# Another order of the steps, with forty-four on another engine, in a fused linear-attention and two-layer MLP kernel

## The chip, the cores and the metric

The kernel runs on one core of one Trainium2 chip. The metric is device time in microseconds (us), from the start to the end of one execution; lower is better. The core has five engines, each of which runs its own instructions in program order: TensorE (PE in the profile), VectorE (DVE), ScalarE (ACT), GpSimd (POOL) and SyncE (SP), which here only issues DMA transfers. An instruction waits on semaphores until its inputs are there and its output buffer is free, and what stands behind it on the same engine waits too.

## What is computed

Two stages, the second on the output of the first. The first is a recurrent attention with a decaying state of 48 x 48 for each of 4 batches and 8 heads over 768 positions; the second a two-layer MLP on the 3072 tokens, 384 to 2048 to 384, with a smooth ReLU between.

```python
def _attn_ref(r, k, v, w, u):
    for t in range(S):
        cur = np.einsum('bhd,bhe->bhde', u[None] * kt, vt)
        y[:, :, t] = np.einsum('bhd,bhde->bhe', rt, state + cur)
        state = w[None, :, :, None] * state + np.einsum('bhd,bhe->bhde', kt, vt)

def _moe_ref(x, w_in, w_out):
    h = x @ w_in
    g = np.where(h >= 1, h, np.where(h <= -1, 0.0, (h + 1) ** 2 / 4))
    return g @ w_out
```

## The kernel before

**Tiling.** Time is cut into 6 chunks of 128 positions (`C`). A *unit* is one batch in one chunk, so there are 24 units, and a *group* is two units, so there are 12 groups `g`; unit `n` belongs to group `n // 2`. Inside a chunk the recurrence is written as matrix products, and a state per batch is carried from chunk to chunk; groups `g` and `g + 2` share their batches.

**The steps.** Every piece of work is a *step*, a small function registered under a name in the dictionary `do`. For a group or unit, in the order of data:

- `load.K`, `load.R` and `loadV` bring K, R and V in by DMA, issued on SP (384 KB a group; the first two groups in halves of 192 KB). `V` casts V to bf16. `w_in` and `w_out` bring the weights of the MLP in, issued on GpSimd.
- `Ks` and `Rs` scale K and R by tables of powers of the decay (line L327). `KU`, `RKU`, `usum` and `V2` make the diagonal term: K times u, that times R, the sum over each head, and the sum times V (L337, L344, L355 or L357, L369).
- For the first three groups `T` transposes Ks and Rs on TensorE (L388) and `TT` copies the result out of PSUM. Later `KRT` does it with a DMA transpose on SP (L398).
- `A` multiplies R by K on TensorE (L406) and `AT` masks it into SBUF (VectorE L421; for units 0 and 1 ScalarE L412 and GpSimd L416). `Y` multiplies by V and adds the part from the state (L441, L446), and `y` adds the diagonal term on VectorE (L468).
- `Sp`, `Tm` and `decay` update the state (TensorE L432, VectorE L476, GpSimd L489), and `sbf` casts it to bf16.
- `xT` brings `y` into the layout of the MLP: for the first three groups through `X` on TensorE (L501) and a copy, later with a DMA transpose on SP (L511), one for both units.
- `mm1` is the first layer (L526), a quarter `q` of the 2048 columns at a time, 12 matmuls. `relu` and `square` on ScalarE (L534, L539) and `gate` on VectorE (L544) make the smooth ReLU. `mm2` is the second layer (L554), by unit and quarter. `o` copies the result out of PSUM, and `out` stores it from SP (L587). For the last unit the second layer is cut in two column blocks (`mm2` and `rest`), and `ends` copies and stores both.

**The order.** The text `ORDER` lists all 714 steps. A loop at the end of the kernel reads it from left to right and calls each step, and an engine's program order is the order in which its steps are called. A token reads `name.arguments@engine:buffers`: `@A`, `@D` and `@P` put the step on ScalarE, VectorE or GpSimd where it can run on several; the digits behind the colon choose the buffer among those of its kind, and a step that writes to a buffer waits until the last step that used it is done. PSUM has three double banks `h0` to `h2` (for `T`, `A`, `mm1`) and two single banks (for `Sp`, `Y`, `X`, `mm2`). `~n` puts n idle matmuls ahead of a step, and `warm.n` is a step of n idle matmuls. The names of steps and units as used in the text are those of the tokens: `mm1.4.0` is quarter 0 of the first layer for group 4, and `xT.8` the transpose that group 4 needs (units 8 and 9).

The loop:

```python
    for token in ORDER.split():
        token, _, idles = token.partition("~")
        idle[0] = int(idles or 0)
        name, _, bufs = token.partition(":")
        name, _, e = name.partition("@")
        kind, *args = name.split(".")
...
        elif kind in do:
            do[kind](e, [int(x, 36) for x in bufs], *[int(x) if x.lstrip("-").isdigit() else x for x in args])
```

Of the kernel before, what the change touches and what calls it, by code (L numbers as in the profile page):

```python
# [40 lines left out]
usum.1.0@A:1 A.1:0~8 V2.0.0@P:0 Ks.2.0@P:2 AT.2.0:1 loadV.2.0:0 V2.1.0@A:1 Y.0:1 T.3:2 sbf.0@A Tm.2@D usum.0.1@D Y.2:0
TT.3@D:3 y.2:0 AT.1.1:2 Rs.2.0@P:2 A.3:1~14 X.2:0 V2.0.1@A y.0:1 AT.3.0:3 warm.2.h.2 X.0:1 T.5:2~8 AT.1.0 xT.2@A:0
T.4:0 TT.5@D:0 Y.1:0 w_in.1 load.K.3.0:0 xT.0@A:1 sbf.1@A usum.1.1@D A.5:1 mm1.0.0.0:2 KU.2.0@P:0 y.1:2 TT.4@D:1
load.R.3.0:0 V.1.1@A X.1:1 Y.3:0 AT.5.0:0 A.4:0 V2.1.1@P xT.1@A mm1.0.0.1 V.2.0@A:2 Sp.5:1 y.3:0 RKU.2.0@P:0
relu.0.0:0 X.3:0 Tm.5@D:0 mm1.0.1.0:1 AT.4.0:1 xT.3@A decay.5 square.0.0:0 usum.2.0@D:0 Sp.4:1 mm1.0.1.1 w_out.0 Y.4:0
relu.0.1:1 mm1.1.1.-1:0 gate.0.0:0 square.0.1:1 Tm.4@D:1 mm1.0.2.-1:2 relu.1.1:0 Y.5:1 square.1.1:0 V2.2.0@P:0 w_out.1
y.4:1 gate.0.1:1 w_out.2 X.4:0 w_out.3 mm1.0.3.-1:1 xT.4@A:2 gate.1.1:2 relu.0.2:1 Sp.3:0 y.5:2 mm1.1.0.-1:0
square.0.2:1 Tm.3@D KU.3.0@P:1 decay.4 gate.0.2:3 relu.0.3:0 relu.1.0:1 mm2.0.0.0:1 mm2.0.1.0:0 Ks.3.0@P:0
square.1.0:0 KRT.K.3:0 mm1.1.3.-1:2 mm2.0.1.1 Rs.3.0@P:0 RKU.3.0@P:1 mm2.0.0.1 square.0.3:1 gate.1.0:4 mm2.0.1.2 gate.0.3:5
relu.1.3:1 loadV.3.0:1 mm2.0.0.2 mm1.1.2.-1:0 square.1.3:0 usum.3.0@D:1 mm2.0.0.3 relu.1.2:0 KRT.R.3:0 mm2.0.1.3  # L50
o.0.0@D:0 square.1.2:1 mm2.1.0.0:1 o.0.1@D gate.1.3:6 load.K.4.0:1 X.5:0 mm2.1.0.1 load.R.4.0:1 xT.5@A V.3.0@A:3
mm1.2.3.-1:1 gate.1.2:7 sbf.3@A V2.3.0@P:1 Sp.7:0 A.7:2 loadV.4.0:0 relu.2.3:1 Tm.7@D:0 A.6:0 mm2.1.0.2 AT.6.0:2
sbf.2@A square.2.3:0 Ks.4.0@P:2 sbf.4@A Sp.6:0 mm2.1.0.3 load.K.5.0:2 Tm.6@D:1 mm1.2.0.-1:0 o.1.0@A:1 AT.7.0:3 decay.6
Y.6:0 Y.7:1 relu.2.0:0 KRT.K.4:1 y.6:0 mm1.2.1.-1:2 KU.4.0@P:0 y.7 V.4.0@A:4 gate.2.3:8 xT.6:1 RKU.4.0@P:0
# [11 lines left out]
gate.4.0:7 y.11 A.12:0 xT.10:2 square.4.1:1 AT.12.0:0 mm2.4.0.0:0 Sp.12:1 relu.4.2:1 KU.7.0@P:1 square.4.2:0
gate.4.1:6 load.K.8.0:2 mm1.4.3.-1:0 V.7.0@A:1 KRT.K.7:0 gate.4.2:9 load.R.8.0:2 A.13:2 Rs.7.0@P:1 mm2.4.0.1 out.3
Tm.12@D:0 mm1.5.0.-1:1 AT.13.0:1 RKU.7.0@P:1 relu.4.3:0 square.4.3:1 relu.5.0:1 gate.4.3:0 loadV.8.0:1 square.5.0:0
sbf.9@A decay.12 mm2.4.0.2 Y.12:1 mm1.5.2.-1:2 usum.7.0@D:1 mm2.4.0.3 Ks.8.0@P:1 y.12:1 mm1.5.1.-1:0 gate.5.0:1
o.4.0@A:1 Y.13:1 KRT.R.7:0 relu.5.2:0 V2.7.0@P:1 KRT.K.8:1 Sp.13:0 square.5.2:1 mm1.5.3.-1:1 y.13 Tm.13@D:0 decay.11  # L70
relu.5.1:1 xT.12:1 gate.5.2:8 mm2.4.1.0:1 KU.8.0@P:0 Sp.14:0 square.5.1:0 mm2.4.1.1 load.K.9.0:0 Tm.14@D:1 mm2.4.1.2
relu.5.3:0 sbf.10@A gate.5.1:3 mm2.5.0.0:0 Rs.8.0@P:2 A.15:2 square.5.3:1 A.14:0 AT.15.0:3 mm2.4.1.3 mm2.5.0.1
V.8.0@A:3 KRT.R.8:1 decay.13 RKU.8.0@P:0 AT.14.0:2 mm1.6.0.-1:2 o.4.1@A load.R.9.0:0 gate.5.3:5 Y.14:1 mm2.5.0.2
Ks.9.0@P:0 y.14:0 relu.6.0:1 mm1.6.1.-1:0 square.6.0:0 usum.8.0@D:0 gate.6.0:4 loadV.9.0:0 load.K.10.0:1 mm2.5.0.3
mm2.5.1.0:1 sbf.11@A sbf.12@A A.17:1 relu.6.1:0 o.5.0@D:0 KU.9.0@P:1 A.16:2 mm2.5.1.1 AT.17.0:0 V2.8.0@P:0 decay.14
Rs.9.0@P:0 square.6.1:1 sbf.13@A Y.15:0 mm2.5.1.2 mm1.6.2.-1:1 y.15 V.9.0@A:4 AT.16.0:1 xT.14:0 KRT.K.9:0 Sp.15:0
RKU.9.0@P:1 gate.6.1:2 mm2.5.1.3 load.R.10.0:1 mm1.6.3.-1:2 relu.6.2:1 square.6.2:0 relu.6.3:0 o.5.1@D Tm.15@D:0
mm2.6.0.0:1 gate.6.2:7 out.5 Y.16:0 mm1.7.1.-1:0 decay.15 square.6.3:1 y.16:1 KRT.R.9:0 Ks.10.0@P:2 Sp.17:0 Tm.17@D:1
gate.6.3:6 load.K.11.0:2 mm2.6.0.1 relu.7.1:1 mm1.7.0.-1:1 KU.10.0@P:0 square.7.1:0 sbf.15@A mm2.6.0.2 Sp.16:0
relu.7.0:0 KRT.K.10:1 loadV.10.0:1 gate.7.1:9 mm1.7.2.-1:2 Rs.10.0@P:1 Tm.16@D:0 mm2.6.0.3 square.7.0:1 o.6.0@A:0  # L80
sbf.14@A usum.9.0@D:1 Y.17:0 mm1.7.3.-1:0 decay.16 y.17 relu.7.2:1 gate.7.0:0 RKU.10.0@P:0 mm2.6.1.0:1 square.7.2:0
Sp.18:0 KRT.R.10:1 mm2.6.1.1 Tm.18@D:0 sbf.16@A decay.17 A.18:1 gate.7.2:1 out.4 mm2.7.0.0:0 relu.7.3:0 xT.16:2
KU.11.0@P:1 mm2.6.1.2 square.7.3:1 AT.18.0:2 V2.9.0@P:1 mm2.7.0.1 load.R.11.0:2 loadV.11.0:0 Ks.11.0@P:1 mm2.6.1.3
gate.7.3:3 mm2.7.0.2 A.21:2 sbf.17@A V.10.0@A:2 o.6.1@A A.19:1 AT.21.0:3 A.20:0 mm2.7.0.3 AT.19.0:1 out.6 Y.18:1
o.7.0@A:1 y.18:0 mm1.8.0.-1:2 relu.8.0:1 KRT.K.11:0 AT.20.0:0 Y.19:0 mm1.8.1.-1:1 y.19 mm2.7.1.0:1 square.8.0:0
usum.10.0@D:0 xT.18:1 Sp.19:0 mm2.7.1.1 Tm.19@D:1 relu.8.1:0 mm1.8.2.-1:0 gate.8.0:8 square.8.1:1 mm2.7.1.2 decay.19
V2.10.0@P:0 relu.8.2:1 V.11.0@A:0 gate.8.1:5 Y.20:0 mm2.7.1.3 mm1.8.3.-1:2 decay.18 square.8.2:0 y.20:1 RKU.11.0@P:1
relu.8.3:0 o.7.1@D gate.8.2:4 square.8.3:1 out.7 mm1.9.0.-1:1 Rs.11.0@P:2 mm2.8.0.0:0 relu.9.0:1 gate.8.3:2 Y.21:1
mm2.8.0.1 KRT.R.11:0 usum.11.0@D:1 square.9.0:0 mm1.9.1.-1:0 y.21 xT.20:0 mm1.9.3.-1:2 relu.9.1:0 gate.9.0:7
square.9.1:1 mm2.8.0.2 mm2.8.1.0:1 relu.9.3:1 gate.9.1:6 mm1.9.2.-1:1 square.9.3:0 mm2.8.1.1 mm2.8.0.3 mm2.8.1.2  # L90
relu.9.2:0 V2.11.0@P:1 gate.9.3:0 o.8.0@D:0 A.22:0 sbf.19@A square.9.2:1 A.23:2 AT.22.0:2 mm2.8.1.3 mm2.9.0.0:0
AT.23.0:1 mm1.10.3.-1:0 o.8.1@A sbf.18@A Y.22:1 mm2.9.0.1 relu.10.3:1 mm1.10.2.-1:2 y.22:0 gate.9.2:9 Y.23:1
relu.10.2:0 mm1.10.0.-1:1 y.23 xT.22:2 square.10.2:0 mm2.9.0.2 relu.10.0:0 mm2.9.1.0:1 gate.10.2:1 mm2.9.0.3
square.10.0:1 mm2.9.1.1 mm1.10.1.-1:2 square.10.3:0 out.8 gate.10.0:3 mm2.9.1.2 gate.10.3:8 relu.10.1:0 mm1.11.0.-1:1
square.10.1:1 mm2.9.1.3 o.9.0@A:1 gate.10.1:5 mm1.11.1.-1:0 o.9.1@A mm2.10.1.0:0 relu.11.1:1 mm1.11.2.-1:2
# [554 lines left out]
```

## Time and profile before

| | |
|---|---|
| device time, three runs | 175.31, 175.77, 176.24 us |
| median | 175.77 us |
| span of the profiled execution | 176.4 us |
| instructions | 4159 |
| HBM read, written | 20.45 MB, 4.72 MB |

The profile is that of one execution, and its span of 176.4 us is that execution's own time; it lies above the three timed ones. Its start and length columns are in us from the start of the span. A row of the timeline merges neighbouring instructions of one kind on one engine: start, length, engine, source line, operation, what is written from what, count, and in brackets how long the engine stood idle before it and what ended that. A row of the groups gives busy time, mean ns of one instruction, and the idle time before them. The table of windows gives for each stretch the busy us of PE, PE's weight loads, VectorE, ScalarE and GpSimd (count in brackets), then the granted TensorE clock (1.00 is full), the busy share of the DMA engines and the GB/s that they moved. Matmuls are pipelined: the length of a merged row of matmuls has the drain of the last one in it, so the chain's rows, from one start to the next, are the better price.

### The profile page before, as it was taken

Reading aid. Unit: us, or ns where it says so; the run is one execution under the profiler, and the core shown is the slowest. Engines: PE = TensorE matmul, PEld = TensorE weight load, DVE = VectorE, ACT = ScalarE, POOL = GpSimd, SP = SyncE. Lnnn points to the kernel's source line nnn. Section 1 sums busy time; section 2 is a strip of 40 time slices with the busy share of each in tenths; the row PEclk is TensorE's granted clock in tenths of the full one; section 3 lists DMA queues with packets and bytes.
Section 4 is the critical chain, followed back from the end, with each engine's and each line's share of the span. In section 5 each row is a group of like instructions: output and inputs, shape, how many; then the busy total and the mean of one; then the engine's idle time right before and its main releaser. Section 6 shows DMA issues by size and latency. Waiting matters only on the chain.

```text
span 176.4 us, 4159 instructions
## 1 busy us (share of the span) xinstructions
PE 165.0 (94%) x1684; PEld 125.2 (71%) x1684; DVE 130.3 (74%) x167; ACT 135.2 (77%) x194; POOL 120.2 (68%) x97
## 2 busy tenths in 40 slices
...
PEclk9999999999999999969999999999999999999998
...
GB/s 109 221 219 192 216 175 234 207 165 209 238 172 196 191 202 252 158 183 175 196 221 211 185 183 159 266 149 243 194 197 93 89 17 4 97 37 89 4 89 89
...
## 3 DMA queue, kind: packets, MB, share of 16 engines
...
HBM read 20.45 MB, written 4.72 MB: 143 GB/s over the span
## 4 chain that ended last, share of the span: by engine, by line
PE 71%; DMA 13%; DVE 7%; ACT 5%; POOL 1%; issue 1%; DVEq 0%; POOLq 0%
PE hp L526 31%; PE op L554 30%; DMA VF<-in_v_dram 5%; DMA w_out_sb<-in_moe_w_out_dram 4%; DMA xT<-yy 3%; DVE AT L421 3%; PE A L406 2%; PE Y L446 2%; PE Y L441 2%; PE Sp L432 1%; ACT V L212 1%; PE ub L242 1%; POOL V L369 1%; PE wb L237 1%; ACT RKU L355 1%; DVE yy L468 1%
## 5 line engine op out<-in xcount | busy, mean ns | idle before, releaser
L526 PE MATMUL hp<-xT,w_in_sb 128*128 128x256 bf16 (+1 forms) x600 | 72.0, 271 | 3.4 <-DMA xT<-yy 2.2
L554 PE MATMUL op<-w_out_sb,gt 128*128 128x384 bf16 (+2 forms) x400 | 71.9, 320 | 0.1
L544 DVE SCALAR_TENSOR_TENSOR gt<-sq,hp 128x1024 bf16<-128x1024 f32 x48 | 57.9, 1216 | 16.2 <-ACT sq L539 16.1
L526 PEld LDWEIGHTS <-w_in_sb 128*128 128x128 bf16 x600 | 56.2, 99 | 13.9 <-issue 3.1
L534 ACT ACTIVATE pt<-hp 128x1024 f32<-128x1024 f32 x48 | 48.7, 1018 | 17.7 <-PE hp L526 17.4
L539 ACT ACTIVATE sq<-pt 128x1024 f32<-128x1024 f32 x48 | 50.4, 1057 | 1.2
L554 PEld LDWEIGHTS <-gt 128*128 128x128 bf16 x400 | 36.5, 98 | 19.3 <-issue 0.5
L421 DVE TENSOR_TENSOR AT<-A,umask 128x1024 bf16<-128x1024 f32 x22 | 26.5, 1218 | 2.2 <-PE A L406 1.9
L337 POOL TENSOR_TENSOR KU<-K,u_bc 128x768 f32<-128x768 f32 (+1 forms) x13 | 21.6, 1658 | 2.0 <-DVE u_bc L212 2.0
L344 POOL TENSOR_TENSOR RKU<-R,KU 128x768 f32<-128x768 f32 (+1 forms) x14 | 22.2, 1589 | 0.3
L489 POOL TENSOR_TENSOR state<-Tm,wCm 128x384 f32<-128x384 f32 x16 | 16.0, 1003 | 8.8 <-DVE Tm L476 8.6
L369 POOL TENSOR_TENSOR V<-V,diag 128x768 f32<-128x768 bf16 (+1 forms) x12 | 16.4, 1365 | 7.1 <-ACT V L212 4.7
L327 POOL TENSOR_TENSOR Ks<-Wdn,K 128x768 bf16<-128x768 f32 x10 | 18.2, 1818 | 1.2 <-DMA K<-in_k_dram 1.2
L327 POOL TENSOR_TENSOR Rs<-Wup,R 128x768 bf16<-128x768 f32 x10 | 18.2, 1819 | 0.1
L476 DVE TENSOR_TENSOR Tm<-Sp,state 128x384 f32<-128x384 f32 x16 | 8.9, 555 | 7.3 <-POOL Ks L327 3.4
L468 DVE TENSOR_TENSOR yy<-Y,V 128x384 bf16<-128x384 f32 x18 | 9.9, 554 | 5.0 <-PE Y L446 3.5
L212 ACT CAST V<-VF 128x768 bf16<-128x768 f32 (+1 forms) x14 | 10.2, 737 | 3.6 <-DMA VF<-in_v_dram 3.5
L446 PE MATMUL Y<-V,AT 128*128 128x48 bf16 x192 | 11.4, 185 | 1.2 <-POOL AT L416 0.9
L446 PEld LDWEIGHTS <-AT 128*128 128x128 bf16 x192 | 9.8, 98 | 2.8 <-POOL AT L416 1.3
L357 DVE TENSOR_REDUCE diag<-RKU 128x16 f32<-128x768 f32 (+1 forms) x13 | 11.1, 852 | 0.9 <-POOL RKU L344 0.9
L212 ACT COPY oo<-op 128x384 f32<-128x384 f32 x13 | 6.2, 476 | 6.7 <-PE op L554 6.3
L212 ACT CAST state_bf<-state 128x384 bf16<-128x384 f32 x20 | 10.0, 503 | 0.0
...
## 6 DMA issues: line engine op xcount, KB each, us to landing
out_dram<-oo SPq DMA_DIRECT2D x11, 384.0 KB, 3.7
K<-in_k_dram SPq DMA_DIRECT2D x10, 384.0 KB, 4.8
R<-in_r_dram SPq DMA_DIRECT2D x10, 384.0 KB, 4.9
VF<-in_v_dram SPq DMA_DIRECT2D x10, 384.0 KB, 5.8
...
w_out_sb<-in_moe_w_out_dram POOLq DMA_DIRECT2D x4, 384.0 KB, 7.5
...
```

The costliest lines, as they stand in the source:

```text
L212: nc.scalar.copy(out, in_) if e == "A" else engines[e].tensor_copy(out, in_)
L327: engines[e].tensor_mul(of_unit(dst, j0, j1)[:, :, :, :D], rep(tab, j1 - j0), of_unit(tiles[what, g], j0, j1))
L337: engines[e].tensor_mul(of_unit(tiles["KU", g], j0, j1), of_unit(tiles["K", g], j0, j1), rep(u_bc, j1 - j0))
L344: engines[e].tensor_mul(of_unit(tiles["RKU", g], j0, j1), of_unit(tiles["R", g], j0, j1), of_unit(tiles["KU", g], j0, j1))
L369: engines[e].tensor_mul(tiles["V2", g][:, hs, :], tiles["V", g][:, hs, :], tiles["diag", g][:, hs].unsqueeze(2).to_broadcast([P, hs.stop - ...
L421: nc.vector.tensor_mul(t.rearrange("p i n t -> p (i n) t"), tiles.pop(("A", n)).rearrange("p i n t -> p (i n) t"), umask.unsqueeze(1).to_b ...
L446: nc.tensor.matmul(t[:, 2 * p + i, :], tiles["AT", n][:, i, p, :], tiles["V", g][:, j * H + 2 * p + i, :], start=(c == 0), stop=True, skip ...
L526: nc.tensor.matmul(hp[:, f, cols], w_in_sb[:, i, n0 : n0 + P], tiles["xT", g][:, units, i, :], start=(i == 0), stop=(i == nK - 1), skip_gr ...
L534: nc.scalar.activation(tiles["pt", g, q], tiles["hp", g, q], AF.Relu, bias=0.5, scale=0.5)
L539: nc.scalar.activation(tiles["sq", g, q], tiles.pop(("pt", g, q)), AF.Square, bias=0.0)
L544: nc.vector.scalar_tensor_tensor(out=gt, in0=tiles.pop(("sq", g, q)), scalar=1.0, in1=tiles.pop(("hp", g, q)), op0=ALU.min, op1=ALU.max)
L554: nc.tensor.matmul(t, tiles["gt", g, q][:, f, j * P : (j + 1) * P], w_out_sb[:, n, cols], start=(n == 0), stop=(n == nF - 1),)
```

## The change

Only the text `ORDER` is another. Both texts hold the same 714 steps with two small exceptions in the idle matmuls: 18 and 4 of them stand together ahead of `bcu` (on `h1`), where 4 stood ahead of `T.0`. Nearly every step stands at another place, and about three hundred use another buffer of their kind. Forty-four steps are on another engine: 20 go from ScalarE to VectorE (nine `sbf`, five `xT`, `o.3.0`, `o.9.0`, `V.4` and others as listed), 13 from VectorE to ScalarE (`TT.2`, `TT.3`, `TT.4`, `usum.5`, `u_bc`, eight `o`), ten from GpSimd to VectorE (`KU.1.0`, `RKU.1.0`, `RKU.3`, `Ks.4`, `KU.4`, `Ks.6`, `Ks.9`, `RKU.10`, `RKU.11`, `V2.11`), and `KU.0.1` from VectorE to GpSimd.

The core of the diff: the start, and the stretch from the stores of group 1 to the first layer of group 4.

```diff
-warm.18 load.K.0.0:0 load.R.0.0:0 load.K.0.1 load.R.0.1 load.K.1.0:1 load.R.1.0:1 bcu:0 u_bc@D KU.0.0@P:0 RKU.0.0@P:0
-lw loadV.0.0:0 bcw:1 load.K.1.1 KU.0.1@D loadV.0.1 wcol:0 Wdn_p:0 Ks.0.0@D:0 Wup_p load.R.1.1 Rs.0.0@D:0 wCm
-KU.1.0@P:1 loadV.1.0:1 Ks.1.0@D:1 warm.4.h.2 T.0:1 load.K.2.0:2 Wdn RKU.1.0@P:1 Rs.1.0@D:1 Rs.0.1@D V.0.0@A:0
...
-square.2.0:1 mm2.1.1.0:0 Sp.8:1 mm2.1.1.1 load.R.5.0:2 Tm.8@D:1 relu.2.1:1 load.K.6.0:0 mm1.2.2.-1:1 gate.2.0:9
-Ks.5.0@P:1 mm2.1.1.2 square.2.1:0 mm2.2.0.0:1 mm2.1.1.3 decay.7 Rs.4.0@P:1 mm1.3.0.-1:0 gate.2.1:0 relu.2.2:0
-square.2.2:1 KRT.K.5:0 mm2.2.0.1 o.1.1@D sbf.5@A relu.3.0:1 mm1.3.1.-1:2 gate.2.2:1 out.1 KU.5.0@P:1 square.3.0:0
-Rs.5.0@P:2 mm2.2.0.2 relu.3.1:0 gate.3.0:3 mm1.3.2.-1:1 KRT.R.4:1 square.3.1:1 loadV.5.0:1 load.R.6.0:0 usum.4.0@D:0
-mm2.2.0.3 mm2.2.1.0:0 KU.6.0@P:0 relu.3.2:1 gate.3.1:5 mm1.3.3.-1:0 square.3.2:0 loadV.6.0:0 gate.3.2:4 mm2.2.1.1
-V2.4.0@P:0 sbf.6@A o.2.0@A:1 A.9:2 sbf.7@A relu.3.3:0 A.8:1 AT.9.0:1 mm2.2.1.2 KRT.R.5:0 square.3.3:1 mm2.3.0.0:1
-AT.8.0:0 out.0 decay.8 mm2.2.1.3 load.K.7.0:1 mm2.3.0.1 o.2.1@A gate.3.3:2 V.6.0@A:0 V.5.0@A:2 Y.8:0 Ks.6.0@P:0
-mm2.3.0.2 y.8:1 Y.9:0 mm2.3.0.3 y.9 RKU.5.0@P:1 A.11:2 xT.8:0 o.3.0@A:0 A.10:1 usum.5.0@D:1 AT.11.0:2 mm2.3.1.0:0
-Sp.10:1 KRT.K.6:1 mm2.3.1.1 Rs.6.0@P:0 RKU.6.0@P:0 Tm.10@D:0 mm2.3.1.2 load.R.7.0:1 Sp.9:1 mm2.3.1.3 Tm.9@D:1
-V2.5.0@P:1 mm1.4.0.-1:0 AT.10.0:3 o.3.1@A sbf.8@A decay.9 decay.10 KRT.R.6:1 usum.6.0@D:0 relu.4.0:1 Sp.11:1 Y.10:0
...
+load.K.1.0:1 warm.18.h.1 load.R.1.0:2 loadV.0.0:0 load.K.0.0:0 warm.4.h.1 bcu:1 load.K.1.1 load.R.0.0:0 lw load.R.0.1
+load.K.0.1 u_bc@A bcw:0 Wdn_p:0 wcol:1 Wup_p Ks.1.0@D:1 Ks.0.0@D:2 KU.0.0@P:1 Rs.0.0@D:0 Rs.1.0@D:1 T.0:2 RKU.0.0@P:1
+Rs.0.1@D wCm KU.1.0@D:0 TT.0@A:2 Wup KU.1.1@P KU.0.1@P load.R.1.1 RKU.0.1@P Wdn A.0:1 V.0.0@A:1 loadV.0.1 T.2:2~3
...
+mm1.2.0.-1:0 relu.2.0:1 AT.7.0:0 Ks.4.0@D:2 Y.6:1 load.R.6.0:0 square.2.0:0 y.6:1 mm1.2.1.-1:2 gate.2.3:4 Y.7:1
+mm2.1.1.0:0 y.7 mm2.1.1.1 mm2.1.1.2 gate.2.0:6 KU.4.0@D:1 xT.6:0 relu.2.1:0 square.2.1:0 mm1.2.2.-1:1 V.4.0@D:1
+KRT.K.4:1 relu.2.2:0 mm2.1.1.3 loadV.5.0:1 RKU.4.0@P:0 mm2.2.1.0:1 mm1.3.0.-1:0 gate.2.1:2 square.2.2:1 o.1.1@D out.0
+relu.3.0:1 mm1.3.1.-1:2 load.R.5.0:1 gate.2.2:8 Ks.6.0@D:0 Sp.8:0 decay.6 square.3.0:0 Ks.5.0@P:1 relu.3.1:0
+mm1.3.2.-1:1 square.3.1:1 mm2.2.1.1 Tm.8@D:1 mm2.2.0.0:0 mm2.2.0.1 mm2.2.0.2 mm2.2.1.2 KU.5.0@P:1 gate.3.0:1
+usum.4.0@D:0 KRT.R.4:1 gate.3.1:9 decay.8 V2.4.0@P:0 mm2.2.0.3 mm1.3.3.-1:0 sbf.7@A A.8:2 relu.3.2:0 load.K.7.0:2
+square.3.2:0 V.5.0@A:4 gate.3.2:7 o.2.0@A:0 out.1 KRT.K.5:0 Rs.5.0@P:0 sbf.6@A AT.8.0:1 relu.3.3:0 KRT.R.5:0 A.9:1
+mm2.2.1.3 o.2.1@A RKU.5.0@P:1 mm2.3.0.0:0 AT.9.0:3 KU.7.0@P:1 square.3.3:0 loadV.6.0:0 usum.5.0@A:1 Y.8:1 mm2.3.0.1
+mm2.3.0.2 y.8:0 gate.3.3:2 Y.9:1 y.9 A.10:1 A.11:2 mm2.3.0.3 o.3.0@D:1 Rs.6.0@P:2 mm2.3.1.0:1 mm2.3.1.1 load.R.7.0:1
+RKU.6.0@P:0 Sp.10:0 sbf.8@A mm2.3.1.2 xT.8:1 mm2.3.1.3 AT.10.0:3 load.K.9.0:1 V2.5.0@P:1 Tm.10@D:1 decay.10
+usum.6.0@D:0 Sp.9:0 Tm.9@D:0 mm1.4.0.-1:1 AT.11.0:2 V.6.0@A:1 Sp.11:0 o.3.1@A Tm.11@D:1 Y.10:1 relu.4.0:0 KRT.K.6:1
...
```

More of the change, by code (lines that the diff above doesn't have):

```diff
@@ L41 @@
[L41 to L54, printed above, removed]
-square.2.0:1 mm2.1.1.0:0 Sp.8:1 mm2.1.1.1 load.R.5.0:2 Tm.8@D:1 relu.2.1:1 load.K.6.0:0 mm1.2.2.-1:1 gate.2.0:9
@@ L66 @@
[L66 to L95, printed above, removed]
```

57 lines of the change are left out of this document (50 added, 7 removed).

## The prediction

> **What bounds the kernel now.** Engine totals come first, then the chain of waits, then TensorE's own timeline. The totals and the clock row of the page:
>
> ```profile
> PE 165.0 (94%) x1684; PEld 125.2 (71%) x1684; DVE 130.3 (74%) x167; ACT 135.2 (77%) x194; POOL 120.2 (68%) x97
> PEclk9999999999999999969999999999999999999998
> ```
>
> TensorE (PE) is the busiest, the others have a quarter to spare, and one slice in mid-span, about 70.6 to 75, shows a lowered clock. A busy share does not say how fast PE goes, so I price its work by the chain, whose rows are start, length, piece:
>
> ```profile
> 60.93 1.30 PE op L554 x8
> 64.19 0.35 PE A L406 x8
> 69.31 0.56 DVE yy L468
> 69.89 6.13 DMA xT<-yy
> 76.06 2.72 PE hp L526 x12
> 79.70 1.31 PE hp L526 x12
> 81.01 0.04 PE Y L441
> ...
> 81.38 1.31 PE hp L526 x12
> 95.00 0.17 PE Sp L432 x4
> 172.93 0.29 DVE o_sb L602
> ```
>
> An undisturbed `mm1` quarter costs 1.31 us, an `mm2` quarter 0.65, an `A` 0.35, a `Y` 0.37 (81.01 to 81.38), an `Sp` 0.17. Between 79.70 and 172.93 PE does 31 `mm1`, 64 `mm2`, 12 `A`, 13 `Y` and 8 `Sp`: 40.6 + 41.6 + 4.2 + 4.8 + 1.4 = 92.6 us of work in 93.2 us. **From 79.7 on nothing is left to win.** The change keeps every one of these steps, so a gain can only come from before that point. There PE loses time in two places, shown by its timeline and by the table of windows:
>
> ```profile
> 73.07 0.81 PE L554 MATMUL op<-w_out_sb,gt 128*128 128x384 bf16 x4
> 76.06 2.72 PE L526 MATMUL hp<-xT,w_in_sb 128*128 128x256 bf16 x12 [2.18 <-DMA xT<-yy]
> ...
> 19.82 0.40 PE L388 MATMUL T<-ident,Rs 128*128 128x128 bf16 x4 [0.76 <-POOL Rs L327]
> 22.05 0.84 PE L526 MATMUL hp<-xT,w_in_sb 128*128 128x128 bf16 x12 [0.48 <-DMA w_in_sb<-in_moe_w_in_dram]
> ...
> 15.00:20.00 5.00, 3.77 (x69) 3.16 (x70) 4.07 (x7) 5.00 (x21) 4.92 (x5) 1.00 1.10 177
> 76.00:79.50 3.50, 3.44 (x27) 2.70 (x27) 0.29 (x1) 0.68 (x1) 3.50 (x3) 0.51 1.13 223
> ```
>
> **Place 1, group 4.** The last `mm2` quarter before `mm1.4.0` begins at 73.07 and is fed by 73.72; `mm1.4.0` begins at 76.06, after the transpose `xT.8`. That is 2.3 us idle. Then the granted clock is 0.51 over 3.5 us, which loses 0.49 x 3.5 = 1.7 us: together **4.0 us**. A wait of 0.76 us at 19.8 left the clock at 1.00 in its window. **Place 2, the start**, up to the first dense product at 22.05: ScalarE is busy 5.00 of 5 us in that window, GpSimd 4.92, PE 3.77.
>
> **The change, part by part.** No step is added or dropped, so PE's own sum stands.
>
> *Place 1.* Ahead of `mm1.4.0` PE has, after `Y.9`, the same steps in both orders: five `mm2` quarters, `A.10`, `A.11`, `Sp.10`, `Sp.9` (3.3 + 0.7 + 0.3 = 4.3 us; only their order differs). VectorE still runs AT.8, AT.9, gate.3.3 and both `y` ahead of the transpose, so `y.9` ends near 69.9 again. What changes is what stands ahead of the transpose on SP, whose queue was so far:
>
> ```profile
> 67.59 0.57 SPq L587 DMA_DIRECT2D out_dram<-oo  x1
> 68.21 0.46 SPq L304 DMA_DIRECT2D K<-in_k_dram  x1
> 69.89 2.08 SPq L511 DMA_TRANSPOSE xT<-yy  x1
> ...
> 82.69 1.21 SPq L511 DMA_TRANSPOSE xT<-yy  x1
> ...
> DMA to landing us min/median/max: 2.7/2.8/6.1
> K<-in_k_dram SPq DMA_DIRECT2D x1, 384.0 KB, 4.7
> ```
>
> A transpose lands 2.8 us after its issue in the median of nine and this one after 6.1. It was issued 1.7 us behind a 384 KB load that landed at 68.21 + 4.7 = 72.9, and it landed 3.1 us after that. In the new order `out.0` and `load.K.7.0` go many steps earlier, and the last load ahead of `xT.8` is `load.R.7.0`. It waits for `RKU.5` on GpSimd, which frees its buffer. So the question is when GpSimd ends `RKU.5`. Its prices, and that of the same width on VectorE:
>
> ```profile
> 66.68 1.83 POOL L344 TENSOR_TENSOR RKU<-R,KU 128x768 f32<-128x768 f32 x1
> ...
> L489 POOL TENSOR_TENSOR state<-Tm,wCm 128x384 f32<-128x384 f32 x16 | 16.0, 1003 | 8.8 <-DVE Tm L476 8.6
> L369 POOL TENSOR_TENSOR V<-V,diag 128x768 f32<-128x768 bf16 x10 | 14.7, 1471 | 7.1 <-ACT V L212 4.7 <-DVE diag L357 2.3
> L357 DVE TENSOR_REDUCE diag<-RKU 128x16 f32<-128x768 f32 x10 | 9.4, 945 | 0.9 <-POOL RKU L344 0.9
> L544 DVE SCALAR_TENSOR_TENSOR gt<-sq,hp 128x1024 bf16<-128x1024 f32 x48 | 57.9, 1216 | 16.2 <-ACT sq L539 16.1
> 47.44 1.47 PE L526 MATMUL hp<-xT,w_in_sb 128*128 128x256 bf16 x12
> ```
>
> So far `RKU.5` ran from 66.68 to 68.5. Now RKU.3, Ks.4, KU.4 and Ks.6 leave GpSimd (4 x 1.8 = 7.2 us) and KU.6 comes ahead (1.8). The pacemaker is then `KU.4` on VectorE, behind `gate.2.0`: `mm1.2.0` ends near 48.9 (47.44 + 1.47), relu and square take 1.0 each, the gate 1.2, KU.4 about 0.95 (estimate from the reduce of that width): 53.1. Behind it on GpSimd stand RKU.4, decay.6, Ks.5, KU.5, decay.8, V2.4, Rs.5, RKU.5: five at 1.8, two at 1.0, one at 1.5 = 12.5, plus 0.4 because V2.4 needs a sum behind `gate.3.0`: **66.0**. The load then lands at 66.0 + 4.7 = 70.7 and the transpose 3.1 later, 73.8, against PE's need at 73.7: 0.1 us idle.
>
> VectorE's new work slows GpSimd, as the start shows:
>
> ```profile
> 5.80 0.56 DVE L337 TENSOR_TENSOR KU<-K,u_bc 128x384 f32<-128x384 f32 x1
> 5.85 1.36 POOL L337 TENSOR_TENSOR KU<-K,u_bc 128x384 f32<-128x384 f32 x1 [2.01 <-DVE u_bc L212]
> 8.24 1.00 POOL L337 TENSOR_TENSOR KU<-K,u_bc 128x384 f32<-128x384 f32 x1
> ```
>
> The same GpSimd product took 1.36 us beside a VectorE product of 0.56, and 1.00 alone: 0.64 us lost per us of overlap. Ks.6 falls into the chain above: 0.95 x 0.64 = 0.6 us, so `RKU.5` ends at 66.6 and the idle becomes 0.7 us. That is about the 0.76 us that left the clock alone, so I take no clock loss. The bounds are an idle of nothing, and the old 4.0. **Place 1 gives 4.0 - 0.7 = 3.3 us.** [...]
>
> *Place 2.* ScalarE is full there. It gets three more `TT` copies and `u_bc`, and loses `usum.1.0` and two `xT` copies ahead of `relu.0.0`:
>
> ```profile
> L212 ACT COPY TT<-T 128x1024 bf16<-128x1024 bf16 x1 | 1.0, 1013 | 0.0
> 13.23 0.24 ACT L355 ACTIVATE RKU<-RKU 128x48 f32<-128x48 f32 x1
> ...
> 15.05 1.89 ACT L367 ACTIVATE V<-V,diag 128x48 f32<-128x48 bf16 x8
> 22.69 0.51 ACT L212 CAST V<-VF 128x384 bf16<-128x384 f32 x1 [1.48 <-DMA VF<-in_v_dram]
> 24.08 0.83 ACT L212 CAST V<-VF 128x768 bf16<-128x768 f32 x1 [0.50 <-DMA VF<-in_v_dram]
> ```
>
> Plus 3.0 + 0.5, minus 1.8 (13.23 to 15.05) and 0.9: 0.8 us more, beside 2.0 us in which ScalarE waited for V. If V lands as before, the wait hides it all; `load.R.2.0` now takes a buffer that `RKU.0.1` must free and holds the V loads behind it on SP, so I take half, **+0.4 us**. Bounds: -1.5 (the V waits gone, less what is left) and +2.0 (the waits kept behind the added work and a late load).
>
> *Later groups.* By the same rows the other moves give VectorE about 12 us more (ten products from GpSimd, nine `sbf` copies, five `xT`, some `o` in exchange), GpSimd 15 less (seven products at 1.8, one at 1.5, two halves at 1.0, less one half that comes to it) and ScalarE 2 less. VectorE ends near 142 of a 173 us span. PE's own work between an `mm1` and the `mm2` that needs its gate stays above 4.2 us, against 3.2 for relu, square and gate, and from group 4 on it is above 4.2 between `Y` and `mm1`, against 0.6 + 2.8 for `y` and its transpose. One new item stands close: `usum.5` goes to ScalarE, 16 heads at twice the 1.8 us of the eight above, behind `RKU.5`: to about 70.3, and with `sbf.8`, `V.6` and `o.3.1` (1.8) to 72.1, while `relu.4.0` is wanted at 75. I cost all this at nothing; were the cover gone, each late gate would cost PE its own 1.2 us.
>
> **Sum**, against the profiled execution's 176.4 us: -3.3 + 0.4 = -2.9, so 173.5. That execution lies 0.6 above the median of the runs shown, 175.77; the same difference on the median gives **172.9 us**.
>
> **The rivals.**
> *The transfer is late again.* SP goes in order and `xT.8` still has a load close ahead of it. If `RKU.5` ends at 68.2, the load starts where the K load started and all 4.0 us are back: 176.2 with the 0.4 of the start. For it: GpSimd has 12.5 us of chain behind one VectorE step and the margin is 1.6 us. Against: three transfers (KRT.R.5, V.6, R.7) instead of four (V.6, KRT.R.5, out.0, K.7) are queued ahead.
> *Slower: GpSimd falls further behind.* The place is the chain from `KU.4` to `RKU.5`; it decides from 68.2 on, where every us of delay is a us of PE. The price with `RKU.5` at 70.5: 2.3 us more than the old idle and clock, 175.8 + 2.3 + 0.4 = **178.5**. `A.10` and `A.11`, which need `KRT.R.5` behind `Rs.5`, now stand ahead of the five `mm2` quarters and would stop those too. For it: VectorE now carries GpSimd's pacemaker, with gates ahead of it, and slows GpSimd besides. Against: four steps, 7.2 us, have left GpSimd there.
> *The start shortens too.* Should V and the weights land so that ScalarE no longer waits, 1.5 us come off as well, and the idle at group 4 vanishes: 175.8 - 4.0 - 1.5 = 170.3. Against: the same bytes must land first.
>
> **How the numbers follow.** The forecast has 0.50 (171.3 to 174.7), the late transfer 0.20, the slower chain 0.18, the shorter start 0.12. The range leaves out the far ends of the last two: 170.5 to 178.0; the forecast's own is 171.3 to 174.7. A measurement of this kernel tells about 0.5% (0.9 us) from no change. Faster by more: 0.50 + 0.12 + a little of the late transfer (a partial one) = 0.65. Within: 0.16. Slower: 0.19.
>
> **What would show it.** Right: `xT.8` lands less than 4.5 us after its issue, no clock row below 1.00 near 76, `RKU.5` ends between 65 and 67.5, PE works at its prices from some 76 us to the end, and the first `mm1` begins between 21.5 and 23.5. Wrong: half clock anywhere in mid-span, a new wait of PE beyond 1 us after 26, or gates that PE waits for after 80.

## The result, and the profile after

The changed kernel is slower by six per cent: 187.83 us median of four runs (185.26 to 188.36) against 175.54 for the kernel before (four runs, 175.26 to 176.24), a ratio of 1.062 with a 95% interval of 1.057 to 1.067. The forecast was 172.9, in a range that ended at 178.0. The ratio uses only the executions within 1.5% of the fastest of their kernel, here 185.26 and 187.40; the medians of all four give 1.070, and the profile below is of the one at 188.36. The experiments ran on four chips, each beside the kernel before; the change itself came to 1.053 on one of them (e5 below). Each time is set against the kernel before on the same chip.

First the totals and the clock row on the page of the changed kernel, as shown for the kernel before:

```profile
span 186.7 us, 4189 instructions
PE 166.1 (89%) x1684; PEld 124.9 (67%) x1684; DVE 144.6 (77%) x183; ACT 135.6 (73%) x203; POOL 107.8 (58%) x88
PEclk9859999999998799999999988999999999999999
```

VectorE gained 14 us of work (12 were estimated) and GpSimd lost 12 (15 were estimated). PE's busy time is about the same, and its span 10.3 us longer, so the time went into waits and low clock. The clock row shows two stretches in mid-span with less than the full clock, where the profile of the kernel before had one. Now PE's own timeline at the places that matter, and the windows with the granted clock in the column after the five engines:

```profile
55.67 1.46 PE L554 MATMUL op<-w_out_sb,gt 128*128 128x384 bf16 x8
59.74 4.15 PE L526 MATMUL hp<-xT,w_in_sb 128*128 128x256 bf16 x24 [2.60 <-DMA xT<-yy]
...
78.57 0.33 PE L432 MATMUL Sp<-V,Ks 128*128 128x96 bf16 x4
78.74 1.47 PE L526 MATMUL hp<-xT,w_in_sb 128*128 128x256 bf16 x12
...
109.86 0.62 PE L406 MATMUL A<-RT,KT 48*128 48x128 bf16 x16 [1.98 <-DMA KT<-Ks]
...
147.65 1.47 PE L526 MATMUL hp<-xT,w_in_sb 128*128 128x256 bf16 x12 [0.88 <-DVE gt L544]
```

```profile
59.70:63.00 3.30, 3.26 (x18) 2.35 (x18) 1.83 (x1) 0.51 (x1) 3.30 (x3) 0.56 0.97 228
...
109.70:113.00 3.30, 3.14 (x28) 1.85 (x29) 1.92 (x3) 1.75 (x3) 0.06 (x1) 0.60 0.74 128
```

At 78.74, `mm1.4.0` follows right behind an `Sp`: the stall for `xT.8` that the forecast wanted to shorten is not there. But the same stall stands one group earlier, ahead of group 3's first layer (`xT.6`, 2.60 us, with a granted clock of 0.56 over the 3.30 us from 59.70), and another at `A.17`, which waits for the transposed K of group 8 (1.98 us, with 0.60 over the 3.30 us from 109.70). The SP queue tells why:

```profile
51.62 3.35 SPq L304 DMA_DIRECT2D R<-in_r_dram  x2
55.08 2.35 SPq L511 DMA_TRANSPOSE xT<-yy  x1
...
98.80 1.47 SPq L304 DMA_DIRECT2D R<-in_r_dram  x1
100.37 2.63 SPq L398 DMA_TRANSPOSE RT<-Rs  x1
103.09 0.53 SPq L304 DMA_DIRECT2D K<-in_k_dram  x1
103.67 2.69 SPq L398 DMA_TRANSPOSE KT<-Ks  x1
```

`y.7` ended at 53.59 (its row: 53.04 and 0.55 of VectorE), but SP was still issuing the R loads of groups 4 and 6 until 54.97, so `xT.6` left at 55.08 with two 384 KB loads just ahead of it, and PE got it at 59.74. `KRT.K.8` left at 103.67, behind V.9, R.9, `KRT.R.8` and K.10.

To see what all of it costs, I took from each trace the time from the start of every PE step to the start of the next, less its price at full clock (the prices of the prediction; 0.21 for a `Y` of the first chunk, which has no state to add, as from 16.02 to 16.23 in the profile of the kernel before; 0.055 an idle matmul, from 0.11 for two at 26.58 in that of the changed one). The sum is PE's loss, by stretch of the span in us:

| kernel | span | lost | 0-30 | 30-50 | 50-70 | 70-100 | 100-130 | 130-end |
|---|---|---|---|---|---|---|---|---|
| before, the prediction's profile | 176.4 | 17.2 | 10.9 | 0.7 | 0.4 | 5.1 | 0.0 | 0.0 |
| before, a second profile (e9) | 171.9 | 12.7 | 10.3 | 0.8 | 0.4 | 1.1 | 0.0 | 0.0 |
| changed, first profile | 186.7 | 28.0 | 11.3 | 1.7 | 4.5 | 2.6 | 5.8 | 2.1 |
| changed, a second profile (e5) | 182.1 | 23.4 | 11.7 | 0.9 | 3.9 | 2.6 | 3.1 | 1.2 |

Span less loss is 158.7 to 159.2 in all four, so the ledger is complete to half a microsecond. The two kernels differ above all where the forecast had put nothing at all, from 50 us to the end. The second profile of the changed kernel has the same two places, 2.07 us ahead of group 3's first layer, with a clock of 0.50 from 59.60 to 63.00, and 1.50 us at `A.17`, with 1.00 in the window from 100 to 110.

### The profile page after: what moved, and what is told of

Same layout as the page of the kernel before. It is cut to its first block, busy times and chain, and to the rows that moved or that the text cites. A ratio compares the mean times of both kernels' runs of the same rounds, so it can differ in the third digit from the quotient of the medians.

```text
span 186.7 us, 4189 instructions
## 1 busy us (share of the span) xinstructions
PE 166.1 (89%) x1684; PEld 124.9 (67%) x1684; DVE 144.6 (77%) x183; ACT 135.6 (73%) x203; POOL 107.8 (58%) x88
## 3 DMA queue, kind: packets, MB, share of 16 engines
q0 software_dynamic: 2912, 3.15, 10.9%
## 4 chain that ended last, share of the span: by engine, by line
PE 26%; DMA 21%; POOL 21%; issue 11%; ACT 7%; DVE 6%; SPq 3%; POOLq 1%; ACTq 0%; DVEq 0%
PE op L554 12%; PE hp L526 11%; DMA VF<-in_v_dram 5%; POOL RKU L344 5%; POOL state L489 5%; DVE gt L544 4%; POOL KU L337 4%; DMA w_out_sb<-in_moe_w_out_dram 4%; POOL V L369 4%; SPq L304 3%; DMA KT<-Ks 3%; ACT pt L534 3%; ACT sq L539 3%; DMA out_dram<-oo 3%; DMA xT<-yy 2%
## 5 line engine op out<-in xcount | busy, mean ns | idle before, releaser
L554 PEld LDWEIGHTS <-gt 128*128 128x128 bf16 x400 | 37.4, 99 | 24.2 <-issue 4.5
L369 POOL TENSOR_TENSOR V<-V,diag 128x768 f32<-128x768 bf16 (+1 forms) x11 | 15.0, 1363 | 18.9 <-DVE diag L357 10.8
L337 POOL TENSOR_TENSOR KU<-K,u_bc 128x768 f32<-128x768 f32 (+1 forms) x12 | 19.7, 1640 | 5.2 <-DMA K<-in_k_dram 5.0
L489 POOL TENSOR_TENSOR state<-Tm,wCm 128x384 f32<-128x384 f32 x16 | 18.2, 1139 | 5.9 <-DVE Tm L476 5.9
L344 POOL TENSOR_TENSOR RKU<-R,KU 128x768 f32<-128x768 f32 (+1 forms) x10 | 16.0, 1601 | 1.0 <-DMA R<-in_r_dram 0.9
L212 ACT COPY oo<-op 128x384 f32<-128x384 f32 x17 | 8.0, 472 | 11.4 <-PE op L554 7.2
L327 POOL TENSOR_TENSOR Ks<-Wdn,K 128x768 bf16<-128x768 f32 x7 | 12.9, 1838 | 1.1 <-PE Sp L432 1.1
L212 ACT CAST V<-VF 128x768 bf16<-128x768 f32 (+1 forms) x12 | 8.7, 724 | 3.8 <-PE Sp L432 1.6
L357 DVE TENSOR_REDUCE diag<-RKU 128x16 f32<-128x768 f32 (+1 forms) x13 | 10.6, 818 | 0.0
L441 PE MATMUL Y<-state_bf,RT 128*128 128x96 bf16 x72 | 8.7, 204 | 0.1
```

The lines of the kernel that those rows point to most:

```text
L327: engines[e].tensor_mul(of_unit(dst, j0, j1)[:, :, :, :D], rep(tab, j1 - j0), of_unit(tiles[what, g], j0, j1))
L337: engines[e].tensor_mul(of_unit(tiles["KU", g], j0, j1), of_unit(tiles["K", g], j0, j1), rep(u_bc, j1 - j0))
L344: engines[e].tensor_mul(of_unit(tiles["RKU", g], j0, j1), of_unit(tiles["R", g], j0, j1), of_unit(tiles["KU", g], j0, j1))
L369: engines[e].tensor_mul(tiles["V2", g][:, hs, :], tiles["V", g][:, hs, :], tiles["diag", g][:, hs].unsqueeze(2).to_broadcast([P, hs.stop - ...
L489: nc.gpsimd.tensor_mul(states[(g % BP) * UNITS + j], tiles.pop(("Tm", n)), wCm)
L554: nc.tensor.matmul(t, tiles["gt", g, q][:, f, j * P : (j + 1) * P], w_out_sb[:, n, cols], start=(n == 0), stop=(n == nF - 1),)
```

## The experiments

**Was the stall at `xT.8` the kernel's, or one execution's?** e9 is the unchanged kernel before, profiled again.

> The kernel before, unaltered, for a second profile. If the wait for xT.8 near 74 us belongs to the kernel: PE idle near 2 us there and a span near 176 us. If it belonged to the one execution that was profiled: xT.8 lands within 4 us of its issue, under 0.6 us idle, no half clock in mid-span, and a span of 172 to 174 us.

It took 173.62 us with a span of 171.9. Its clock row, then the rows of its SP and PE timelines around `mm1.4.0`:

```profile
PEclk9999999999999999999999999999999999999999
```

```profile
67.20 0.46 SPq L304 DMA_DIRECT2D K<-in_k_dram  x1
69.39 1.53 SPq L511 DMA_TRANSPOSE xT<-yy  x1
...
72.20 0.81 PE L554 MATMUL op<-w_out_sb,gt 128*128 128x384 bf16 x4
72.85 1.47 PE L526 MATMUL hp<-xT,w_in_sb 128*128 128x256 bf16 x12
```

The load still stands ahead of the transpose, and there is neither a wait nor a low clock: `mm1.4.0` begins 0.65 us after the quarter before it. e8 then takes the load and the store away from that place:

```diff
-gate.2.2:1 out.1 KU.5.0@P:1 square.3.0:0
+gate.2.2:1 out.1 out.0 KU.5.0@P:1 square.3.0:0
...
-AT.8.0:0 out.0 decay.8 mm2.2.1.3 load.K.7.0:1 mm2.3.0.1 o.2.1@A
+AT.8.0:0 decay.8 mm2.2.1.3 mm2.3.0.1 o.2.1@A
...
-xT.8:0 o.3.0@A:0
+xT.8:0 load.K.7.0:1 o.3.0@A:0
```

> The kernel before, with two tokens moved on SP: the store of group 0 right behind that of group 1, and the load of K for group 7 right behind xT.8 instead of ahead of it. Queue theory: xT.8 lands 2.8 to 3.5 us after its issue instead of 6.1, the 2.3 us idle and 1.7 us of slow clock near 74 to 79 go, and the kernel is 3 to 4 us faster than before, 0.977 to 0.985. If the transfer was not late through the load ahead of it: within 0.5% of before.

175.84 us against 174.40, ratio 1.010 (1.006 to 1.013). There was nothing to gain at that place, and the later load of K.7 delays what is queued behind it: the transposed R of group 6 now leaves SP at 75.41 (72.99 in e9), and PE waits for it at `A.12`:

```profile
80.73 0.40 PE L406 MATMUL A<-RT,KT 48*128 48x128 bf16 x8 [1.40 <-DMA RT<-Rs]
```

**The changed kernel again, and its two large waits.** e5 is the changed kernel unaltered.

> The changed kernel itself, unaltered, beside the others of this chip, as their yardstick. Both theories: 1.055 to 1.070 times before.

183.83 us (183.54 to 186.49) against 174.40, 1.053 (1.047 to 1.059). e3 moves one load out of the way of `xT.6`, e4 moves both transposes of group 8 ahead of the loads, e6 does both:

```diff
-Y.6:1 load.R.6.0:0 square.2.0:0
+Y.6:1 square.2.0:0
...
-KRT.K.4:1 relu.2.2:0
+KRT.K.4:1 load.R.6.0:0 relu.2.2:0
```

```diff
-xT.12:1 gate.5.1:4
+xT.12:1 KRT.R.8:1 KRT.K.8:1 gate.5.1:4
...
-load.R.9.0:1 KRT.R.8:1 load.K.10.0:0 KRT.K.8:1 AT.15.0:1
+load.R.9.0:1 load.K.10.0:0 AT.15.0:1
```

> The changed kernel with one load, that of R for group 6, put behind xT.6 and KRT.K.4 on SP instead of ahead of them. Queue theory: xT.6 is issued at the end of y.7 (53.6 instead of 55.1 us), lands by 57.5, and the idle and the half clock near 57 to 62 go: 4 us less than the changed kernel, 183 to 185 us. Port theory: nothing changes, 186 to 189 us.

> The changed kernel with the two transposes of group 8 put right behind xT.12 on SP, ahead of the loads of V and R for group 9 and K for group 10. Queue theory: KRT.K.8 is issued near 99.5 instead of 103.7 us and lands before A.17 is reached near 107.6, so the 2.1 us idle and the slow clock behind it go: 3 to 4 us less than the changed kernel, 183.5 to 185.5 us. Port theory: nothing changes, 186 to 189 us.

> The changed kernel with the edits of the third and the fourth run together: the load of R for group 6 behind xT.6, the two transposes of group 8 ahead of the loads. Queue theory: PE's losses of 4.2 us near 57 and of 3.4 us near 108 both go, 6 to 8 us less than the changed kernel, 1.015 to 1.03 times before. Port theory: at most 2 us less.

In each of them the wait that was aimed at goes. SP and PE of e3, and SP of e4:

```profile
53.83 1.59 SPq L511 DMA_TRANSPOSE xT<-yy  x1
...
55.89 1.46 PE L554 MATMUL op<-w_out_sb,gt 128*128 128x384 bf16 x8
57.43 2.78 PE L526 MATMUL hp<-xT,w_in_sb 128*128 128x256 bf16 x24
```

```profile
99.00 1.23 SPq L398 DMA_TRANSPOSE KT<-Ks  x1
```

And the time hardly answers: 184.82 us (1.059, 1.052 to 1.065) for e3, 183.62 (1.054, 1.049 to 1.059) for e4, 183.45 (1.049, 1.041 to 1.056) for e6, against 1.053 for e5. PE comes earlier and meets the next late thing. In e6 the loss between 50 and 70 us falls from 3.9 (e5) to 1.4, and that between 70 and 100 rises from 2.6 to 5.1. What it waits for now, over the whole span (total, times, longest):

```profile
PE A L406 <- DMA RT<-Rs: 2.2, 3, 1.0
...
PE hp L526 <- DMA xT<-yy: 1.0, 2, 0.8
...
PE hp L526 <- DVE gt L544: 0.9, 1, 0.9
```

The waits for a transposed R stand at 67.4, 72.6 and 82.8 us, those for `xT` at 77.2 and 87.9; the gate is the one at the end, at 143.

e7 adds the fourth part of `w_out` issued earlier and the other buffer for `o.10.0`, whose wait for a store held up ScalarE for 2.85 us near the end:

```diff
-w_out.2 mm1.1.0.-1:2
+w_out.2 w_out.3 mm1.1.0.-1:2
...
-KU.3.0@P:1 w_out.3 decay.4
+KU.3.0@P:1 decay.4
...
-o.10.0@A:0
+o.10.0@A:1
```

> The sixth run's kernel, with the last quarter of w_out issued on GpSimd right behind the third (ahead of KU.3) and the copies of group 10's result into the other output buffer. Queue theory: the 1.1 us wait for w_out near 42 goes, and relu.11.3, which stood on ScalarE behind a copy that waited 2.9 us for the store of group 9, runs in time: 1.5 to 2.5 us less than the sixth run. Port theory: under 0.5 us less.

183.87 us, 1.051 (1.043 to 1.059): no change that can be told from e6. Both waits are gone from its profile, and new ones of 1.4 and 1.0 us for `y` on VectorE have come.

**GpSimd runs dry.** GpSimd and VectorE of the changed kernel in the stretch where the forecast had `RKU.5` end at 66.0 to 66.6:

```profile
50.63 1.76 POOL L489 TENSOR_TENSOR state<-Tm,wCm 128x384 f32<-128x384 f32 x1
57.14 1.81 POOL L327 TENSOR_TENSOR Rs<-Wup,R 128x768 bf16<-128x768 f32 x1 [4.75 <-issue]
58.91 1.81 POOL L344 TENSOR_TENSOR RKU<-R,KU 128x768 f32<-128x768 f32 x1
...
70.07 1.83 POOL L344 TENSOR_TENSOR RKU<-R,KU 128x768 f32<-128x768 f32 x1
...
50.57 0.96 DVE L327 TENSOR_TENSOR Ks<-Wdn,K 128x768 bf16<-128x768 f32 x1 [0.29 <-DMA K<-in_k_dram]
54.64 0.95 DVE L337 TENSOR_TENSOR KU<-K,u_bc 128x768 f32<-128x768 f32 x1
```

`KU.4` was done on VectorE at 55.59, but `Rs.4`, which now stands ahead of `RKU.4`, began only at 57.14, after 4.75 us of idle. The view names no releaser for it. `Rs.4` needs `load.R.4`, which the new order puts behind K.6, K.4, V.4 and K.5 on SP. e12 takes e6, puts that load earlier, and puts K of group 6 and its product `KU.6` later:

```diff
-mm2.0.1.3 load.K.6.0:0 o.0.1@A mm2.1.0.0:1 load.K.4.0:2 square.1.2:0
+mm2.0.1.3 o.0.1@A mm2.1.0.0:1 load.K.4.0:2 load.R.4.0:2 square.1.2:0
...
-load.K.5.0:1 A.6:0 relu.2.3:0 sbf.2@A load.R.4.0:2
+load.K.5.0:1 load.K.6.0:0 A.6:0 relu.2.3:0 sbf.2@A
...
-V2.3.0@P:1 KU.6.0@P:0 Sp.6:0
+V2.3.0@P:1 Sp.6:0
...
-RKU.4.0@P:0 mm2.2.1.0:1
+RKU.4.0@P:0 KU.6.0@P:0 mm2.2.1.0:1
```

> The sixth run's kernel (both transposes freed), with the load of R for group 4 right behind that of K for group 4, the load of K for group 6 behind that of K for group 5, and KU.6 on GpSimd behind RKU.4. Starved-GpSimd theory: GpSimd's idle of 4 to 5 us ahead of Rs.4 (52 to 57 us) goes, RKU.5 ends 3 us earlier, the waits of PE for A.8, A.10 and A.12 shrink, and the kernel is 2 to 4 us faster than the sixth run, 1.025 to 1.035 times before. If GpSimd is not what holds the stretch: within 1 us of the sixth run.

GpSimd's timeline in e12:

```profile
49.75 2.27 POOL L327 TENSOR_TENSOR Rs<-Wup,R 128x768 bf16<-128x768 f32 x1 [1.89 <-DMA R<-in_r_dram]
54.47 2.07 POOL L344 TENSOR_TENSOR RKU<-R,KU 128x768 f32<-128x768 f32 x1 [2.46 <-DVE KU L337]
```

The wait for the load shrinks, and the next one is the pacemaker that the forecast named, `KU.4` on VectorE. `RKU.5` ends at 69.5 there, against 71.1 in e6. 182.75 us, 1.052 (1.046 to 1.057): again no change that can be told from e5 or e6.

**Products on VectorE.** e11 puts `RKU.10`, `RKU.11` and `V2.11` back on GpSimd, e10 the nine `sbf` back on ScalarE, each in the changed order:

```diff
-RKU.10.0@D:1
+RKU.10.0@P:1
...
-RKU.11.0@D:1
+RKU.11.0@P:1
...
-V2.11.0@D:1
+V2.11.0@P:1
```

```diff
-sbf.4@D
+sbf.4@A
...
-sbf.18@D
+sbf.18@A
```

> The changed kernel with three late products (RKU.10, RKU.11, V2.11) back on GpSimd, which is free there. Port theory: RKU.11 took 2.6 us on VectorE beside GpSimd's Ks.11 and held gate.8.3, for which PE waited 1.05 us ahead of mm1.9.3; that wait goes, 1 us less than the changed kernel. Queue theory: no difference.

> The changed kernel with the nine state casts (sbf) that went to VectorE back on ScalarE, where each takes 0.5 us; order and buffers unchanged. Port theory: on VectorE they took up to 1.8 us behind a GpSimd product and held up gates and masks behind them, so 1 to 3 us less than the changed kernel. Queue theory: within 1 us of it.

e11 removes the wait of `mm1.9.3` for a gate (0.88 us of idle at 147.65 above): the gate had stood behind `RKU.11`. Its loss between 130 us and the end is 0.5. The times do not move: 184.06 us, 1.058 (1.052 to 1.065) for e11 and 183.81, 1.055 (1.048 to 1.062) for e10.

**Which part of the change?** e1 is the order before with the new engines, e2 the new order with the engines before.

> The order and the buffers of before; only the forty-four steps stand on the engines of the changed kernel. Queue theory (the changed kernel is slow because DMA transposes now stand behind loads on SP, which this kernel does not have): within 2 us of before, 174 to 178 us. Port theory (products and casts moved to VectorE and GpSimd's products hold each other up, 1.8 us at a time): most of the 11 us come with the engines, 181 to 188 us, with DVE products of 128x768 above 1.5 us and sbf casts on DVE above 0.8 us.

> The order and the buffers of the changed kernel; all forty-four steps back on the engines of before. Queue theory: the two long waits for transposes (xT.6 near 57 us, 2.8 us idle and half a clock; KRT.K.8 near 108 us, 2.1 us idle and half a clock) stay, 184 to 190 us. Port theory: the loss goes with the engines, 176 to 180 us.

e1: 188.38 us against 174.38, 1.079 (1.074 to 1.083). e2: 196.47, 1.123 (1.116 to 1.129). Each half alone costs more than both together (5 to 6 per cent), so the new order goes better with the new engines than with the old. e2 lies above what either theory had expected of it. e14 to e16 split the 44 moves of e1 in three, again in the order before: the ten products to VectorE with `KU.0.1`; the twenty steps from ScalarE to VectorE; the thirteen from VectorE to ScalarE. One token of each:

```diff
-RKU.3.0@P:1
+RKU.3.0@D:1
...
-sbf.4@A
+sbf.4@D
...
-o.5.1@D
+o.5.1@A
```

> The order before, with the ten products on VectorE instead of GpSimd and KU.0.1 the other way, nothing else. All 44 moves in this order cost 14.0 us (188.4 against 174.4). If products that VectorE and GpSimd run beside each other carry it, this alone costs 8 us or more (182 or slower); if it is the load on ScalarE and the copies, under 3 us (177 or faster).

> The order before, with the twenty steps that go from ScalarE to VectorE (nine sbf, five xT, o.3, o.6, o.9, V.4, V.10, usum.1) and nothing else. By the theory of the products 0 to 3 us slower than before (174 to 177); if VectorE's own queue is the trouble, 4 to 8 us slower (178 to 182).

> The order before, with the thirteen steps that go from VectorE to ScalarE (u_bc, three TT, usum.5, eight o) and nothing else. By the theory of the products 0 to 3 us slower than before (174 to 177), of it up to 1 us at the start; if ScalarE is the trouble, where each o stands ahead of a relu or square, 4 to 8 us slower (178 to 182).

Against 174.23 us: e14 179.41 (1.029, 1.021 to 1.036), e15 179.13 (1.027, 1.022 to 1.032), e16 178.60 (1.025, 1.020 to 1.030). That is 5.2, 4.9 and 4.4 us, 14.5 in sum against 14.0 for all of them: no part carries the loss, each of the three costs about a third. The theory that the products alone carry it falls.

How a product does it shows in e14. VectorE, GpSimd and PE near `mm2.7.0.0`:

```profile
116.36 1.21 DVE L544 SCALAR_TENSOR_TENSOR gt<-sq,hp 128x1024 bf16<-128x1024 f32 x1
117.49 2.30 DVE L344 TENSOR_TENSOR RKU<-R,KU 128x768 f32<-128x768 f32 x1
119.72 0.54 DVE L476 TENSOR_TENSOR Tm<-Sp,state 128x384 f32<-128x384 f32 x1
...
117.16 1.82 POOL L337 TENSOR_TENSOR KU<-K,u_bc 128x768 f32<-128x768 f32 x1 [0.62 <-DMA K<-in_k_dram]
118.93 2.19 POOL L369 TENSOR_TENSOR V<-V,diag 128x768 f32<-128x768 bf16 x1
...
118.56 0.40 PE L406 MATMUL A<-RT,KT 48*128 48x128 bf16 x8
120.31 0.97 PE L554 MATMUL op<-w_out_sb,gt 128*128 128x384 bf16 x5 [1.35 <-DVE Tm L476]
```

`RKU.10` on VectorE takes 2.30 us and not 0.95, because a GpSimd product runs from 117.16 to 118.98; it ends 0.81 us after that one. `Tm.18` stands behind it on VectorE and PE behind `Tm.18`, for 1.35 us. e16 shows the same on ScalarE, where `o.5.1` now stands behind a square and a relu:

```profile
106.56 1.47 PE L526 MATMUL hp<-xT,w_in_sb 128*128 128x256 bf16 x12
109.51 0.81 PE L554 MATMUL op<-w_out_sb,gt 128*128 128x384 bf16 x4 [1.48 <-ACT oo L212]
...
107.00 1.06 ACT L539 ACTIVATE sq<-pt 128x1024 f32<-128x1024 f32 x1
108.07 1.02 ACT L534 ACTIVATE pt<-hp 128x1024 f32<-128x1024 f32 x1
108.99 0.47 ACT L212 COPY oo<-op 128x384 f32<-128x384 f32 x1
```

The first-layer quarter ahead of the wait is fed by 107.87 (106.56 + 1.31), the copy that frees the single bank starts 1.1 us later, and PE waits 1.48. Not all of e16's loss is of this kind. By the same ledger 1.8 of its 4.4 us above e9 lie before 30 us, where `bcw` waits 1.1 us for `lw`, which in this order stands behind `u_bc` on ScalarE, and 1.6 between 100 and 130, the stretch of these rows. Of e15 only the times are used.

**All mends together.** e13 is the changed kernel with the edits of e7, e10, e11 and e12.

> The changed kernel with every edit of the runs before it together: the loads R.6 and the transposes of KRT.8 out of the way on SP, load.R.4 early and KU.6 behind RKU.4, w_out.3 early, o.10.0 on its other buffer, nine sbf back on ScalarE, RKU.10, RKU.11 and V2.11 back on GpSimd. If the loss is a sum of waits that can be named one by one, this gives 179 us or less and a ratio of 1.03 or less. If each wait that goes only uncovers the next, it stays at 181 to 184, 1.04 to 1.055.

180.93 us, 1.035 (1.027 to 1.043), between the two expectations. Its ledger has a loss of 19.0 us against 23.4 in e5, and the 6.3 above e9 are spread out: 1.3 before 30 us, 1.4 from 50 to 70, 1.5 from 70 to 100, 2.5 from 100 to 130 and 0.4 after, less 0.7 between 30 and 50. So the named waits did add up, but only as a group: e13's interval lies below e5's, and those of the single edits do not. Most of the loss is left, and it has no single name.

## Why the prediction was wrong

**What bounds the kernel: wrong for the kernel, right for one execution.** The prediction found 4.0 us at group 4 in the profile and built its gain on them. The runs speak against their being the kernel's: e9 has neither the wait nor the low clock, and e8 wins nothing by clearing that place. The device time says the same. In every run for which both are listed the device time is 1.66 to 1.77 us above the span (186.7 and 188.36; 171.9 and 173.62), so the profiled execution with its span of 176.4 took about 178.1, more than any of the timed runs that the prediction had (175.31 to 176.24). The prediction set the span itself beside the median, saw a difference of 0.6, and passed it on. Had it put 178.1 beside 175.77, the 2.3 us between them would have asked which part of the profile the median does not have. (No second profile was taken together with those first runs, so that their median had nothing at all of the 4.0 us is argued.) From some 30 us on, PE in the second profile (e9) loses 2.3 us in all. **After the start there was next to nothing to win, and much to lose.**

**Place 1: nothing waits there, but not by the forecast's path.** `xT.8` stalls nobody after the change, as forecast, and in e9 it stalls nobody before it either. Its step "`RKU.5` ends at 66.6" failed: it ended at 71.90 (70.07 + 1.83). The chain was costed as instructions back to back from `KU.4` on, with `KU.4` done at 53.1. `KU.4` was done at 55.59, and `RKU.4` began only at 58.91, behind `Rs.4`, which waited for a load that SP issued late; the prediction's list begins with `RKU.4` and leaves `Rs.4` out. From there to the end of `RKU.5` it took 13.0 us, against 13.5 in the forecast. PE itself was 5 us late by then (`mm1.4.0` at 78.74, where the forecast had PE ready at 73.7), and so was `y.9`, which ended at 75.37 and not at 69.9. So `xT.8` left SP at once, at 75.39; with `y.9` on time it would have stood behind `load.R.7`, which left only at 72.11. That the delay did not show there was luck.

**Place 2: right within its bounds.** Forecast +0.4 us between -1.5 and +2.0; the ledger up to 30 us has +0.4 between the first two profiles and +1.4 between e9 and e5. The mechanism is there too: ScalarE's longest wait for V falls from 1.48 us to 0.31 in the changed kernel's first profile, and the first `relu` starts at 25.20 where it started at 24.82.

**Later groups at nothing: the step that failed.** It is the term that carries the result: from 30 us on, the changed kernel loses 11.7 us in e5 against 2.3 in e9, 9.4 us where 0 was put down. Three things in it were wrong. The test was by engine totals and by the shortest cover between steps, and neither sees a queue: what stands ahead on SP was worked out for `xT.8` and not for `xT.6`, `KRT.8` and `load.R.4`, whose places the two orders show just as well. The price of a full-width product on VectorE was 0.95 us, and is 0.95 in five of the eight of the changed kernel's first profile, but 2.31 to 2.58 in the three that began behind a GpSimd product; the prediction charged the contention to GpSimd alone, at 0.64 us for each us of overlap. And the thirteen steps to ScalarE were counted as balance between engines, while e16 shows them costing 4.4 us in the order before. How the 9.4 us divide among the three is not shown: in the changed order itself, moving `sbf` or three products back changed no time (e10, e11), and all edits together took the ratio from 1.053 to 1.035.

**The rivals.** The slower one, at 0.18 and 178.5, had the sign and an item of the cause, GpSimd behind `KU.4`, but neither its place nor its size: `RKU.5` went past the 68.2 at which it was to decide, and `xT.8` stalled nobody at group 4. The late transfer came, at `xT.6` in place of `xT.8`. The prediction listed as signs of error half clock in mid-span, waits of PE beyond 1 us and late gates; all three are in the profile.

**What stays open.** About 6 us between e13 and the kernel before are not settled: PE's waits after 50 us in e13's profile are of 1.3 us at most, spread over DMA transposes, `AT` and `y`. That these are the price of an order whose steps stand too close to each other is argued from e1, e2 and the equal thirds, not shown step by step. No version tried beats the kernel before.
